# An FNet layer with a gated MLP on one core: a new order of products at the end, x added by DMA, and two jobs of MLP1 moved

## The chip, the core and the metric

The kernel runs on one core of a Trainium2 chip. The core has TensorE for matmuls (PE in the profile, its weight loads PEld), VectorE (DVE), ScalarE (ACT), GpSimd (POOL) and SyncE (SP), which work on their own instruction lists in parallel and wait for each other through semaphores. SP, ACT and POOL can issue DMA transfers; the letter q behind a name (SPq, ACTq, POOLq) stands for an engine's DMA issues. The metric is the device time of one execution in microseconds (us); lower is better.

## The reference

For an input x of 2048 rows (tokens) and 512 columns:

```python
xn = layernorm(x)                       # over the columns
a, b = xn @ dft_hid_re.T, xn @ dft_hid_im.T
s = dft_seq_re @ a - dft_seq_im @ b     # FNet mixing, [2048, 512]
h = relu(xn @ w1 + b1) ** 2             # w1: [512, 1792]
g = silu(h @ w2 + b2)                   # w2: [1792, 512]
out = x + s * g
```

All of it is in float32.

## The kernel before, in words

Every matmul operand is split into a high and a low part (float32r), and a product is made of three matmuls: high by high, high by low, low by high. ScalarE writes the high part (L125), VectorE the low one by subtraction (L128), which it can do only when ScalarE has finished. On top of that the large products are cut into blocks of two by two and multiplied with seven block products instead of eight (Winograd's form of Strassen's method). Each operand therefore needs sums of its blocks (VectorE, L257 to L269) before its split, and each result needs a few additions of products.

The work runs in four stages: the DFT over the sequence (until about 331 us), the DFT over the columns (Y units, until about 418 us), MLP1 (28 units, until about 561 us) and MLP2 with the gate and the output (until the end).

**MLP1.** Unit n = 0 to 27 makes 256 hidden features for a chunk of 512 tokens: chunk c = n // 7, feature part p = n % 7. A unit has seven products of six matmuls, in the regions A, B, C and D of PSUM (two sets of banks, for even and odd units). TensorE's order overlaps two units; in the loop of unit n it does product 1 of n, products 5 and 4 of n − 1, products 7 and 6 of n, product 3 of n − 1, product 2 of n. ScalarE copies A into B (`seed` "B") and B into C (`seed` "C"), since several results share partial sums. VectorE takes the results from B and C (c22, c21, L775) and squares them (L790); product 3 then adds into region B, so it must wait until c22 has read B. Likewise product 5 adds into B and must wait until ScalarE's seed has copied B to C.

Beside this, VectorE and ScalarE must prepare the operands of later units. Each such job is a generator with a letter and a number, and one call of `go` makes its next step: V (a part of w1: load, sums, split), x (normalized tokens of a chunk, half 0 or 1: load, normalization L610 and sums, split), w (a part of w2), m (the rows of mean and scale for a chunk), h (hidden features back from DRAM as operand of MLP2), l (a load). The table `H_SIDE` says for each unit which steps are called at which of three places: before c22 and c21 of the unit before (first), behind them (second), and at the unit's end (later). An engine runs its instructions strictly in the order in which they were written, so the table sets what stands behind what on VectorE, ScalarE and SP.

**MLP2.** For each chunk of 512 tokens, seven products (banks m1 to m7) are summed over the parts p = 0 to 6 (`outer`, L811). For the last chunk product 4 has two banks of its own, one for each half of its columns (`m4[0]`, `m4[1]`). A part's operand g is made by `operand` in one of three buffers by turns, so a new one waits until TensorE has used the one three parts ago. `REST` says from which part on the last chunk's products are kept for the end, to be done product by product, so that the results come one after another: C11 (from products 1, 2), C22 (1, 2, 6, 7, 5), C12 and C21, each 256 by 256, in a tile z of 128 partitions. Each result then goes through `silu` (ScalarE), `times` (VectorE, with s from the first stages, kept in DRAM and loaded by `load_fin`) and `plus` (VectorE, adds x, and SP sends it out). For the first chunks two of the four results get x in another way: `finish` issues a DMA from POOL's queue that adds x from DRAM onto the tile in SBUF (`accum_op=ALU.add`, L846), and `put` (L849) sends the tile out once that DMA is done.

In the last chunk before the change, x is added to C12 by POOL instead of VectorE (L863 with `eng=nc.gpsimd`), and C21 is finished in two halves.

Of the kernel before, what the change touches and what calls it, by code (L numbers as in the profile page):

```python
# [9 lines left out]
F32R = mybir.dt.float32r  # L10
AF = mybir.ActivationFunctionType
ALU = mybir.AluOpType

P = 128
S, D, F = 2048, 512, 1792
NS, ND, NF = S // P, D // P, F // P
NJ, NP = NS // 2, NF // 2
CW = 256
NC = S // CW
TC = 512  # L20
NTC = S // TC
# [2 lines left out]

ASIDE = 4.2

REST = NP - 3

W1_EARLY = (0, 1)
W2_LATE = (4, 5)  # L30
# [25 lines left out]
H_SIDE = {  # L56
    0: ((), ("V2", "x2"), ("x3",)),
    1: (("V4",), ("V3",), ("V5",)),
    2: ((), ("V4", "V5"), ("V6",)),
    3: ((), ("x3", "V5"), ("m2",)),  # L60
    4: ((), ("V6", "x2"), ("x4",)),
    5: ((), ("V6", "x3"), ("w4",)),
    6: ((), ("x3",), ("x5",)),
    7: (("w4",), ("w4",), ("w5",)),
    8: ((), ("x4",), ()),
# [10 lines left out]
    21: (("h1",), (), ()),  # L76
    22: (("w1",), ("h0",), ("w2",)),
    23: ((), ("h1",), ("w3",)),
    24: (("w2",), ("w1",), ("w6", "h2")),
    25: (("w3",), ("w2",), ("h3", "l4")),  # L80
    26: (("w6",), ("w3",), ("l5",)),
    27: (("h2",), (), ()),
}
ACT_PAIR = (7, 10, 13, 15, 17, 18, 19, 20, 26)
O_SIDE = {0: (("h4",), ("h5",)), 1: ((), ("w6",))}
# [28 lines left out]
C21, C11, C22, C12 = range(4)  # L114
# [5 lines left out]
def fnet_gated_kernel(ctx, tc, x, xt, ct, wd, w1, w2, b1, b2, out):  # L120
    nc = tc.nc
# [8 lines left out]
    def split(*parts):  # L130
        split_hi(*parts)
        split_lo(*parts)
# [211 lines left out]
    one, two = slice(0, 1), slice(1, 2)  # L344
# [112 lines left out]
    g = plain_parts(0, 1)  # L457
# [7 lines left out]
    for j in range(1, NJ):  # L465
# [15 lines left out]
        g = plain_parts(*order[j + 1])  # L481
# [62 lines left out]
    for n, s in enumerate(steps):  # L544
        c, j = s
        if j == 0:
            ms = {k: bank(tag, f"m{k}_{c}") for k, tag in
                  {1: "bb", 2: "b20", 6: "b21", 3: "b30", 5: "b31", 7: "b32", 4: ("ba", "bc")[c % 2]}.items()}
        g = part.pop(s)
# [22 lines left out]
        if j == NJ - 1:  # L572
            e = buf("e", [P, 2048], f"c{c}")
# [9 lines left out]
    xT, W1, W2, fin, ready = {}, {}, {}, {}, {}  # L583
# [83 lines left out]
    def operand(n):  # L667

        apart = n in (0, 1, 3)
        if apart:  # L670
            x_, t = (buf(f"pq{n % 3}{i}", [P, 4, 256], f"hr{n}_{i}") for i in range(2))
        else:
            e = buf("u" if n % 4 else "wd0", [P, 8, 256], f"hr{n}")
            x_, t = e[:, 4:8], e[:, 0:4]
        nc.sync.dma_start(x_, HD[divmod(n, NP)])
        yield
        sums_rows(t, x_)
        yield
        g = ready[n] = buf(("xc6", "xc7", "xc4")[n % 3], [P, 2, 7, 256], f"g{n}", F32R)
        for s, src in ((slice(0, 4), t), (slice(4, 7), x_[:, 0:3])) if apart else ((slice(0, 7), e[:, 0:7]),):  # L680
            split(g[:, HI, s], g[:, LO, s], src)
        yield

    makers.update(m=load_rows, x=tokens, k=load_w1, l=load_w2, V=make_w1, w=make_w2, h=operand)


# [118 lines left out]
    def outer(m, k, n, cols=(0, 1)):  # L805

        p = n % NP
        a, b = PRODUCTS[k]
        for i in cols:
            for a_, b_ in PASSES:  # L810
                nc.tensor.matmul(m[:, i * 256:(i + 1) * 256], ready[n][:, a_, H_SLOT[a], i * P:(i + 1) * P],  # L811
                                 W2[p][:, b_, b], start=p == 0 and i == 0 and (a_, b_) == (HI, HI) and k not in BIASED,
                                 stop=p == NP - 1 and (a_, b_) == (LO, HI), skip_group_check=True)
# [4 lines left out]
    def at(src, k):  # L818

        h, b = WHERE[k]  # L820
        return src.rearrange("(h k p) (b e) -> h b p k e", h=2, k=2, b=2)[h, b]
# [14 lines left out]
    def finish(c, e, k):  # L836

        if len(fin[c]) > 2 + k // 2:
            silu(e, k)
            times(c, e, k)  # L840
            plus(c, e, k)
            return
        silu(e, k)
        times(c, e, k)
        z = e[:, k].rearrange("p (k e) -> p k e", e=256)
        nc.gpsimd.dma_start(z, at(x[c * TC:(c + 1) * TC], k), accum_op=ALU.add)  # L846

    def put(c, e, k):
        nc.sync.dma_start(at(out[c * TC:(c + 1) * TC], k), e[:, k].rearrange("p (k e) -> p k e", e=256))  # L849

    def silu(e, k, cols=slice(0, 2)):

        z = e[:, k, cols.start * 256:cols.stop * 256]
        nc.scalar.activation(z, z, AF.Silu)

    def times(c, e, k, cols=slice(0, 2)):
        w = slice(cols.start * 256, cols.stop * 256)
        nc.vector.tensor_tensor(e[:, k, w], e[:, k, w], fin[c][k // 2][:, k % 2, w], op=ALU.mult)

    def plus(c, e, k, cols=slice(0, 2), eng=None):  # L860
        w = slice(cols.start * 256, cols.stop * 256)
        z = e[:, k, w]
        (eng or nc.vector).tensor_tensor(z, z, fin[c][2 + k // 2][:, k % 2, w], op=ALU.add)  # L863
        nc.sync.dma_start(at(out[c * TC:(c + 1) * TC], k)[:, cols], z.rearrange("p (k e) -> p k e", e=256))

    go("m0")
# [23 lines left out]
    for u in range(1, NC):  # L890
        n = 2 * u + 2
# [40 lines left out]
    for n in range(NTC * NP):  # L932
# [17 lines left out]
        if n == NTC * NP - 1:  # L950
            ms = Banks(0)
# [22 lines left out]
    for n in range(NTC * NP):  # L974
        c, p = divmod(n, NP)
        last = c == NTC - 1
        if n and not last and p == 0:

            ms = Banks(c)
            for k in (2, 4, 5):  # L980
                bias(ms[k], k)
        elif last and p == 0:

            ms = {k: bank(t, f"m{k}_last") for k, t in
                  {1: "b20", 2: "b21", 6: "b30", 7: "b31", 5: "bb", 3: "ba"}.items()}
            m4 = bank("bc", "m40_last"), bank("b32", "m41_last")
# [5 lines left out]
        def add(k, p):  # L992
            if last and k == 4:
                for i in range(2):
                    outer(m4[i], k, NP * c + p, (i,))
            else:
                outer(ms[k], k, NP * c + p)

        go(*O_SIDE.get(n, ((), ()))[0])
        if n == 1:  # L1000
            for k, i in ((1, 1), (2, 1), (6, 1), (4, 1), (5, 0), (3, 0), (7, 1), (5, 1), (3, 1)):
                add(k, i)
        elif n and (not last or p < REST):
            for k in ORDER if p else FIRST_LAST if last else FIRST:
# [28 lines left out]
    def rest(ks, ps=range(REST, NP)):  # L1033
        for k in ks:
            for f in ps:
                add(k, f)

    def step(to, a, b, op, w=whole):
        nc.vector.tensor_tensor(e[:, to, w], a[:, w], e[:, b, w], op=op)

    rest((1, 2, 6), range(REST, tail))
    rest((1, 2), (tail,))
    nc.scalar.activation(e[:, C21], ms[1], AF.Copy)
    step(C11, ms[2], C21, ALU.add)
    silu(e, C11)
    times(c, e, C11)
    plus(c, e, C11)
    rest((6,), (tail,))
    rest((7,))
    step(C12, ms[6], C21, ALU.add)  # L1050
    step(C21, ms[7], C12, ALU.subtract)
    rest((5,))
    step(C22, ms[5], C21, ALU.add)
    silu(e, C22)
    step(C12, ms[5], C12, ALU.subtract)
    rest((3,))
    for f in range(REST, NP):
        outer(m4[0], 4, NP * c + f, (0,))
    times(c, e, C22)
    step(C12, ms[3], C12, ALU.add)  # L1060
    silu(e, C12)
    plus(c, e, C22)
    step(C21, m4[0], C21, ALU.subtract, w[0])
    silu(e, C21, one)
    for f in range(REST, NP):
        outer(m4[1], 4, NP * c + f, (1,))
    times(c, e, C12)
    plus(c, e, C12, eng=nc.gpsimd)
    step(C21, m4[1], C21, ALU.subtract, w[1])
    silu(e, C21, two)  # L1070
    times(c, e, C21, one)
    plus(c, e, C21, one)
    times(c, e, C21, two)
    plus(c, e, C21, two)

# [42 lines left out]
```

## Time and profile before

| What | Value |
|---|---|
| Device time, median of three runs (lowest to highest) | 705.83 us (705.46 to 707.34) |
| Profiled execution | 707.13 us |
| Its span, from first to last instruction | 705.4 us |
| Granted TensorE clock over the span | 0.998 |
| TensorE busy | 695.8 us (99%) |
| VectorE busy | 606.8 us (86%) |
| ScalarE busy | 357.9 us (51%) |
| Matmuls | 5440 |

A row of the timeline gives the start and the duration in us, the engine, the line of the kernel, the operation, the tile written and the tiles read, the shape and the number of instructions merged into the row. Brackets at its end give the idle time of the engine before it and who ended it. In a row of waits come the waiting engine and line, the releaser, the total, the number of times and the longest. In a row of DMA issues come the queue, the count, the size of one and the time from issue to landing.

### The profile page before, as it was taken

The numbers are of one execution on the slowest core, as the hardware profiler recorded it, in microseconds if no ns is written. First come the engines' busy times: TensorE is split into PE (matmuls) and PEld (weight loads), VectorE is DVE, ScalarE is ACT, GpSimd is POOL, SyncE is SP. The second block draws the span as 40 slices with busy tenths as digits, with TensorE's granted clock in tenths as the row PEclk, the third lists the DMA queues.
The fourth block names the chain that finished last, engine by engine and source line by source line (L and its number), as shares of the span: only waits on it lengthen the run. The fifth ranks groups of instructions, "written<-read, shape, count | busy, mean of one in ns | idle before, by whom it ended". The sixth has DMA issues, their size and how long they took to land.

```text
span 705.4 us, 13138 instructions
## 1 busy us (share of the span) xinstructions
PE 695.8 (99%) x5440; PEld 671.7 (95%) x5440; DVE 606.8 (86%) x848; ACT 357.9 (51%) x474; POOL 6.5 (1%) x9
## 2 busy tenths in 40 slices
PE   9999999999999999999999999999999999999996
PEld 6778889999999999999999999999999999999996
DVE  7999779999988988888898699999648599989896
ACT  4446544444434333344455458677778664444441
POOL 0000000000000000000000000000000000101000
PEclk9999999999999999999999999999999999999999
DMA  8535755667475544276587446587426955666743
GB/s 302 190 109 189 269 203 209 247 214 278 174 282 200 184 163 176 94 281 230 176 297 266 151 168 214 204 318 259 157 119 200 356 163 203 185 204 186 235 143 130
DMA packets 50619, 146.88 MB, mean 208 GB/s; under 512 B 4864, under 2 KB 19200, under 8 KB 49152
## 3 DMA queue, kind: packets, MB, share of 16 engines
q1 hardware_dynamic: 43264, 126.13, 51.6%
q10 hardware_dynamic: 6208, 18.88, 6.8%
q0 software_dynamic: 1088, 1.05, 1.0%
q8 instruction: 42, 0.69, 0.4%
q14 instruction: 17, 0.14, 0.1%
HBM read 99.88 MB, written 46.15 MB: 207 GB/s over the span
## 4 chain that ended last, share of the span: by engine, by line
PE 93%; DVE 4%; DMA 1%; ACT 1%; issue 1%; DVEq 0%; ACTq 0%
PE m L325 33%; PE m_o L811 15%; PE r_B L705 12%; PE r_A L705 8%; PE pq_b L340 8%; PE m_last L811 5%; PE r_C L705 4%; PE r_D L705 4%; PE pq_ba L340 2%; PE pq_bb L340 1%; PE pq_bc L340 1%; DMA w2raw<-in_w 1%; DVE c L306 1%; DVE yg L128 0%; DMA x<-in_x 0%
## 5 line engine op out<-in xcount | busy, mean ns | idle before, releaser
L325 PEld LDWEIGHTS m<-g,xc 128*128 128x128 f32 x2016 | 236.4, 188 | 0.5 <-DVE g L128 0.2
L325 PE MATMUL m<-g,xc 128*128 128x256 f32 x2016 | 236.8, 279 | 0.0
L125 ACT ACTIVATE g<-u 128x1792 fp32r<-128x1792 f32 (+3 forms) x70 | 100.1, 1430 | 145.6 <-PE m L325 55.6
L128 DVE TENSOR_TENSOR g<-u,g 128x1792 fp32r<-128x1792 f32 (+3 forms) x70 | 117.5, 1679 | 27.0 <-ACT g L125 26.8
L811 PE MATMUL m_o<-w,g 128*128 128x256 f32 x882 | 105.8, 282 | 0.0
L811 PEld LDWEIGHTS m_o<-w,g 128*128 128x128 f32 x882 | 105.5, 191 | 0.0
L125 ACT ACTIVATE g<-hr 128x1792 fp32r<-128x1792 f32 (+2 forms) x31 | 47.9, 1556 | 49.5 <-PE m_o L811 31.4
L705 PE MATMUL r_B<-xT,w 128*128 128x256 f32 x504 | 70.3, 283 | 0.8 <-DVE h L775 0.8
L340 PE MATMUL pq_b<-g,xc 128*128 128x512 f32 x240 | 66.8, 397 | 0.2
L705 PEld LDWEIGHTS r_B<-xT,w 128*128 128x128 f32 x504 | 64.4, 190 | 1.4 <-DVE h L775 1.1
L128 DVE TENSOR_TENSOR g<-hr,g 128x1792 fp32r<-128x1792 f32 (+2 forms) x31 | 56.8, 1839 | 7.9 <-ACT g L125 7.9
L340 PEld LDWEIGHTS pq_b<-g,xc 128*128 128x128 f32 x240 | 43.8, 188 | 13.2 <-ACT xc L125 2.3
L705 PE MATMUL r_A<-xT,w 128*128 128x256 f32 x336 | 45.0, 282 | 1.3 <-DVE w L128 1.3
L705 PEld LDWEIGHTS r_A<-xT,w 128*128 128x128 f32 x336 | 42.1, 190 | 1.5 <-DVE w L128 1.5
L705 PE MATMUL r_B<-wdp,yg 128*128 128x256 f32 x288 | 37.5, 283 | 0.2 <-DVE y L715 0.2
L705 PEld LDWEIGHTS r_B<-wdp,yg 128*128 128x128 f32 x288 | 35.6, 190 | 0.6 <-DVE y L715 0.4
L811 PE MATMUL m_last<-w,g 128*128 128x256 f32 x294 | 35.3, 282 | 0.0
L811 PEld LDWEIGHTS m_last<-w,g 128*128 128x128 f32 x294 | 35.2, 191 | 0.0
L257 DVE TENSOR_TENSOR u<-u 128x512 f32<-128x512 f32 x48 | 32.9, 685 | 1.9 <-DMA u<-in_ct 1.9
L128 DVE TENSOR_TENSOR yg<-yraw,yg 128x1792 fp32r<-128x1792 f32 x13 | 26.2, 2020 | 3.8 <-ACT yg L125 3.8
L306 DVE TENSOR_TENSOR c<-m,c 128x512 f32<-128x512 f32 x42 | 27.2, 685 | 1.7 <-PE m L325 1.0
L125 ACT ACTIVATE yg<-yraw 128x1792 fp32r<-128x1792 f32 x13 | 22.1, 1697 | 6.6 <-DVE yraw L266 5.2
(172 smaller groups left out, 865.4 us busy)
## 6 DMA issues: line engine op xcount, KB each, us to landing
u<-in_ct SPq DMA_DIRECT2D x63, 512.0 KB, 3.6
hd<-h ACTq DMA_DIRECT2D x28, 512.0 KB, 4.1
hr<-hd SPq DMA_DIRECT2D x28, 512.0 KB, 3.7
wdp<-wdd SPq DMA_DIRECT2D x8, 896.0 KB, 6.5
yraw<-pqd SPq DMA_DIRECT2D x13, 512.0 KB, 5.1
pqd<-c SPq DMA_DIRECT2D x6, 1024.0 KB, 4.0
y<-y ACTq DMA_DIRECT2D x8, 512.0 KB, 4.3
fin<-y SPq DMA_DIRECT2D x16, 256.0 KB, 5.1
```

What stands on the lines that cost most here:

```text
L125: nc.scalar.activation(hi, src, AF.Copy)
L128: nc.vector.tensor_tensor(lo, src, hi.bitcast(F32), op=ALU.subtract)
L257: nc.vector.tensor_tensor(t[:, 0:2], r[:, 0:1].to_broadcast([P, 2, 256]), r[:, 1:3], op=ALU.add)
L306: nc.vector.tensor_tensor(part_(to), m, part_(frm), op=op)
L325: nc.tensor.matmul(ps[:, d], w[:, a_, d * P:(d + 1) * P], halves(mv(b_)), start=first and d == 0 and (a_, b_) == (HI, HI), stop=last and ( ...
L340: nc.tensor.matmul(accs[c][k], w, part[c, j][:, b_, 2 * h:2 * h + 2], start=j == 0 and h == 0 and (a_, b_) == (HI, HI), stop=j == NJ - 1 a ...
L705: nc.tensor.matmul(self.region(REGION[k]), w, mv, start=i == 0 and k in (1, 7), stop=i == len(ops) - 1, skip_group_check=True)
L811: nc.tensor.matmul(m[:, i * 256:(i + 1) * 256], ready[n][:, a_, H_SLOT[a], i * P:(i + 1) * P], W2[p][:, b_, b], start=p == 0 and i == 0 an ...
```

## The change

Four things change.

1. `REST` goes from `NP - 3` to `NP - 4`: in the last chunk the products of parts 3, 4, 5 and 6 are kept for the end. Four operands live at once then, so the last one gets a fourth buffer (wd0). For parts 3 to 5 the products 1, 2, 6, 7 and 5 are done part by part, then part 6 product by product, then products 3 and 4.
2. C11 and C22 of the last chunk get x by an accumulating DMA from POOL (`add_x`); they are sent out later by `put`, C11 by SP's queue and C22 by ScalarE's. C12 gets x from VectorE; POOL makes no addition any more.
3. For the second half of C21, the earlier result is subtracted from the bank `m4[1]` in PSUM (VectorE) while product 4's last part is still missing; TensorE adds that part afterwards, and ScalarE takes silu straight from the bank.
4. `H_SIDE`: in units 2 to 5, x3's normalization moves to unit 2, weight part 6 (V6) does its sums and its split in unit 4, before x2's split, and the rows m2 are loaded a unit earlier. In units 24 to 27 the steps of w2's parts move from the first place to the second, behind the split of the part before.

```diff
-REST = NP - 3
+REST = NP - 4
...
 H_SIDE = {
-    2: ((), ("V4", "V5"), ("V6",)),
-    3: ((), ("x3", "V5"), ("m2",)),
+    2: ((), ("V4", "V5", "x3"), ("V6", "m2")),
+    3: ((), ("V5",), ()),
...
-        g = ready[n] = buf(("xc6", "xc7", "xc4")[n % 3], [P, 2, 7, 256], f"g{n}", F32R)
+        g = ready[n] = buf("wd0" if n == NTC * NP - 1 else ("xc6", "xc7", "xc4")[n % 3], [P, 2, 7, 256], f"g{n}", F32R)
...
+    def add_x(c, e, k):
         z = e[:, k].rearrange("p (k e) -> p k e", e=256)
         nc.gpsimd.dma_start(z, at(x[c * TC:(c + 1) * TC], k), accum_op=ALU.add)
...
-    rest((1, 2, 6), range(REST, tail))
+    def rest4(i, ps):
+        for f in ps:
+            outer(m4[i], 4, NP * c + f, (i,))
+
+    for f in range(REST, tail):
+        rest((1, 2, 6, 7, 5), (f,))
     rest((1, 2), (tail,))
     nc.scalar.activation(e[:, C21], ms[1], AF.Copy)
     step(C11, ms[2], C21, ALU.add)
     silu(e, C11)
+    rest((6, 7, 5), (tail,))
+    step(C12, ms[6], C21, ALU.add)
     times(c, e, C11)
-    plus(c, e, C11)
-    rest((6,), (tail,))
-    rest((7,))
-    step(C12, ms[6], C21, ALU.add)
+    add_x(c, e, C11)
     step(C21, ms[7], C12, ALU.subtract)
-    rest((5,))
     step(C22, ms[5], C21, ALU.add)
     silu(e, C22)
     step(C12, ms[5], C12, ALU.subtract)
+    times(c, e, C22)
+    add_x(c, e, C22)
     rest((3,))
-    for f in range(REST, NP):
-        outer(m4[0], 4, NP * c + f, (0,))
-    times(c, e, C22)
     step(C12, ms[3], C12, ALU.add)
     silu(e, C12)
-    plus(c, e, C22)
+    rest4(1, range(REST, tail))
+    nc.vector.tensor_tensor(m4[1][:, w[1]], m4[1][:, w[1]], e[:, C21, w[1]], op=ALU.subtract)
+    put(c, e, C11)
+    times(c, e, C12)
+    plus(c, e, C12)
+    rest4(0, range(REST, NP))
+    rest4(1, (tail,))
     step(C21, m4[0], C21, ALU.subtract, w[0])
     silu(e, C21, one)
-    for f in range(REST, NP):
-        outer(m4[1], 4, NP * c + f, (1,))
-    times(c, e, C12)
-    plus(c, e, C12, eng=nc.gpsimd)
-    step(C21, m4[1], C21, ALU.subtract, w[1])
-    silu(e, C21, two)
+    nc.scalar.activation(e[:, C21, w[1]], m4[1][:, w[1]], AF.Silu)
     times(c, e, C21, one)
     plus(c, e, C21, one)
+    put(c, e, C22, nc.scalar)
     times(c, e, C21, two)
     plus(c, e, C21, two)
```

Three places show how the order moves. The first is VectorE in units 2 to 4. In the rows, w1raw is a raw part of w1 with its sums, w_5 and w_6 are split parts, xr_4455 is x3 (in xs are its sums), xT_4680 and xT_4744 are x2's split operand, and each h tile holds two units' results (h_4559 and h_4561: units 2 and 3). Before, from the sums of part 5 on:

```order
L266 TENSOR_TENSOR w1raw_4519<-w1raw_4519 128x256
L775 SCALAR_TENSOR_TENSOR h_4559<-r_B,b1s,h_4559 128x256
L775 SCALAR_TENSOR_TENSOR h_4559<-r_C,b1s,h_4559 128x256
L790 SCALAR_TENSOR_TENSOR h_4559<-h_4559 128x2x256
L610 TENSOR_TENSOR xr_4455<-xr_4455,rows_4191 128x1024 x2
L128 TENSOR_TENSOR w_5_4613<-w1raw_4519,w_5_4613 128x1792
```

And after the change:

```order
L266 TENSOR_TENSOR w1raw_4519<-w1raw_4519 128x256
L610 TENSOR_TENSOR xr_4455<-xr_4455,rows_4191 128x1024 x2
L775 SCALAR_TENSOR_TENSOR h_4561<-r_B,b1s,h_4561 128x256
L775 SCALAR_TENSOR_TENSOR h_4561<-r_C,b1s,h_4561 128x256
L790 SCALAR_TENSOR_TENSOR h_4561<-h_4561 128x2x256
L128 TENSOR_TENSOR w_5_4618<-w1raw_4519,w_5_4618 128x1792
```

The two L610 of x3 now stand ahead of unit 2's c22, c21 and square.

The second place is ScalarE in unit 4. Its rows begin with the seed of B for unit 4 and c11 of unit 3 (L763); `h<-r_D` is unit 4's copy of product 7, `r_C<-r_B` its seed of C. Before:

```order
L135 ACTIVATE r_B<-r_A 128x256
L763 ACTIVATE h_4559<-r_A,b1s 128x256
L125 ACTIVATE xT_4680<-xr_4244 128x768
L125 ACTIVATE xT_4680<-xs_4414 128x1024
L135 ACTIVATE h_4692<-r_D 128x256
L135 ACTIVATE r_C<-r_B 128x256
```

And after:

```order
L135 ACTIVATE r_B<-r_A 128x256
L763 ACTIVATE h_4561<-r_A,b1s 128x256
L125 ACTIVATE w_6_4680<-w1raw_4586 128x1792
L135 ACTIVATE h_4690<-r_D 128x256
L135 ACTIVATE r_C<-r_B 128x256
```

The split of part 6, which reads sums that VectorE makes in the same unit behind unit 3's c22, c21 and square, now stands ahead of unit 4's copy and seed; x2's split moves a unit back.

The third place is VectorE in unit 24 (h_5826 holds unit 23's results, w2raw_1_5852 the sums of w2's part 2, w_1 the split of part 1). The difference, with the rows of before marked by − and those of after by +:

```order
+L775 SCALAR_TENSOR_TENSOR h_5826<-r_B,b1s,h_5826 128x256
+L775 SCALAR_TENSOR_TENSOR h_5826<-r_C,b1s,h_5826 128x256
+L790 SCALAR_TENSOR_TENSOR h_5826<-h_5826 128x2x256
+L128 TENSOR_TENSOR w_1_5943<-w2raw_5298,w_1_5943 128x1792
 L257 TENSOR_TENSOR w2raw_1_5852<-w2raw_0_5851 128x512
 L258 TENSOR_TENSOR w2raw_1_5852<-w2raw_1_5852,w2raw_0_5851 128x256
 L259 TENSOR_TENSOR w2raw_1_5852<-w2raw_1_5852,w2raw_0_5851 128x256
-L775 SCALAR_TENSOR_TENSOR h_5826<-r_B,b1s,h_5826 128x256
-L775 SCALAR_TENSOR_TENSOR h_5826<-r_C,b1s,h_5826 128x256
-L790 SCALAR_TENSOR_TENSOR h_5826<-h_5826 128x2x256
-L128 TENSOR_TENSOR w_1_5946<-w2raw_5298,w_1_5946 128x1792
```

The sums of part 2 now come behind unit 23's steps and the split of part 1.

At the end of the program POOL has two more L849 transfers in the place of its addition, each waiting only for loads and for VectorE's multiply of its tile.

More of the change, by code (lines that the diff above doesn't have):

```diff
@@ L58 @@
     1: (("V4",), ("V3",), ("V5",)),
-    2: ((), ("V4", "V5"), ("V6",)),
-    3: ((), ("x3", "V5"), ("m2",)),
-    4: ((), ("V6", "x2"), ("x4",)),
-    5: ((), ("V6", "x3"), ("w4",)),
+    2: ((), ("V4", "V5", "x3"), ("V6", "m2")),
+    3: ((), ("V5",), ()),
+    4: ((), ("V6", "V6"), ("x4", "w4")),
+    5: ((), ("x2", "x3"), ()),
     6: ((), ("x3",), ("x5",)),
@@ L78 @@
     23: ((), ("h1",), ("w3",)),
[L79 to L82, printed above, removed]
+    24: ((), ("w1", "w2"), ("w6", "h2")),
+    25: ((), ("w2", "w3"), ("h3", "l4")),
+    26: ((), ("w3", "w6"), ("l5",)),
+    27: ((), ("h2",), ()),
 }
@@ L844, in finish, with put @@
         times(c, e, k)
+        add_x(c, e, k)
+    def add_x(c, e, k):
         z = e[:, k].rearrange("p (k e) -> p k e", e=256)
         nc.gpsimd.dma_start(z, at(x[c * TC:(c + 1) * TC], k), accum_op=ALU.add)
-    def put(c, e, k):
-        nc.sync.dma_start(at(out[c * TC:(c + 1) * TC], k), e[:, k].rearrange("p (k e) -> p k e", e=256))
+    def put(c, e, k, queue=nc.sync):
+        queue.dma_start(at(out[c * TC:(c + 1) * TC], k), e[:, k].rearrange("p (k e) -> p k e", e=256))
     def silu(e, k, cols=slice(0, 2)):
@@ L858, in times, with plus @@
         nc.vector.tensor_tensor(e[:, k, w], e[:, k, w], fin[c][k // 2][:, k % 2, w], op=ALU.mult)
-    def plus(c, e, k, cols=slice(0, 2), eng=None):
+    def plus(c, e, k, cols=slice(0, 2)):
         w = slice(cols.start * 256, cols.stop * 256)
         z = e[:, k, w]
-        (eng or nc.vector).tensor_tensor(z, z, fin[c][2 + k // 2][:, k % 2, w], op=ALU.add)
+        nc.vector.tensor_tensor(z, z, fin[c][2 + k // 2][:, k % 2, w], op=ALU.add)
         nc.sync.dma_start(at(out[c * TC:(c + 1) * TC], k)[:, cols], z.rearrange("p (k e) -> p k e", e=256))
```

## The prediction

> **What bounds the kernel now.** I read the page's busy shares first, then the waits of TensorE, then the timeline of the three places where the change moves work: early MLP1, late MLP1 and the end.
>
> ```profile
> PE 695.8 (99%) x5440; PEld 671.7 (95%) x5440; DVE 606.8 (86%) x848; ACT 357.9 (51%) x474; POOL 6.5 (1%) x9
> PE r_A L705 <- DVE w L128: 1.3, 1, 1.3
> 664.25 35.25 PE L811 MATMUL m_last<-w,g 128*128 128x256 f32 x294
> ```
>
> TensorE is busy 695.8 of 705.4 us and the change neither adds nor removes a matmul. So it can move the time only by TensorE's waits in MLP1 (the wait above, and one on r_B shown further down, lie in the units that the table reorders) and by what runs after the last matmul. The last row gives the pace: 35.25/294 = 0.12 us a matmul, 0.72 for a product of six, 5.04 for a unit of 42.
>
> **Early MLP1, before.** All rows are the timeline's: start, duration, engine, line.
>
> ```profile
> 430.03 0.42 DVE L266 TENSOR_TENSOR w1raw<-w1raw 128x256 f32<-128x256 f32 x1
> 430.37 0.48 DVE L775 SCALAR_TENSOR_TENSOR h<-r_B,b1s,h 128x256 f32<-128x256 f32 x1
> 431.31 1.60 PE L705 MATMUL r_B<-xT,w 128*128 128x256 f32 x12
> 432.08 2.48 DVE L610 TENSOR_TENSOR xr<-xr,rows 128x1024 f32<-128x1024 f32 x2
> 434.48 2.02 DVE L128 TENSOR_TENSOR w<-w1raw,w 128x1792 fp32r<-128x1792 f32 x1
> 438.12 0.69 DVE L263 TENSOR_TENSOR w1raw<-w1raw 128x512 f32<-128x512 f32 x1
> 439.30 0.42 DVE L266 TENSOR_TENSOR w1raw<-w1raw 128x256 f32<-128x256 f32 x1
> 439.23 0.88 PE L705 MATMUL r_B<-xT,w 128*128 128x256 f32 x6
> 440.17 1.70 ACT L125 ACTIVATE w<-w1raw 128x1792 fp32r<-128x1792 f32 x1
> 441.76 0.38 ACT L135 ACTIVATE h<-r_D 128x256 f32<-128x256 f32 x1
> 445.43 0.74 PE L705 MATMUL r_A<-xT,w 128*128 128x256 f32 x4 [1.32 <-DVE w L128]
> 450.99 0.87 PE L705 MATMUL r_B<-xT,w 128*128 128x256 f32 x6
> ```
>
> See here that VectorE works back to back, one piece behind TensorE, and that TensorE then starves once, at 445.43, for weight 6. From product 5 of unit 4 (439.23) to that of unit 6 (450.99) are 11.76 us, where two units need 10.08: 1.68 lost.
>
> *Step 1, x3's normalization moved ahead of unit 2's c22.* The two L610 take 434.48 − 432.08 = 2.40 of VectorE. c22, at 430.37 before, comes at 432.77 and ends at 433.25. TensorE's product 3 of unit 2, the second half of the twelve at 431.31, is due at 432.03 and adds into the bank that c22 reads; it starts at 433.30: +1.27. Behind it ScalarE's c12, square and seed shift alike, which nobody else is short of.
>
> *Step 2, weight 6 summed and split in one unit.* The sums still stand behind unit 3's three steps, so they run at 438.23 to 439.84 (0.1 later than before). But ScalarE's split of weight 6 now stands at ScalarE's place of 435, and waits for the sums until 439.88, then takes 1.70. Queued behind it are the m7 copy (0.26 to 0.36 a step) and unit 4's seed of C from B, which would end near 442.15. TensorE's product 5 of unit 4 overwrites B and must wait for that seed: due at 439.23 + 1.27 = 440.50, it starts at 442.2, +1.70. VectorE idles meanwhile (439.84 to 441.6) and the split's low part ends at 443.55.
>
> *Step 3, what is gained.* Weight 6 is needed at 446.5 now, so the 1.68 go. x3's operand is later, 451.45 for the first half by the same durations; unit 7 asks for it at 452.0, with 0.5 to spare. From product 5 of unit 4 on: 442.2 + 10.08 = 452.28 against 450.99. Steps 1 to 3: **+1.29**. Bounds: −1.68 if ScalarE's and VectorE's lateness is absorbed, +1.9 if x3's second half (452.6) is what unit 7 waits for; I take the worked value, the only one with every row behind it.
>
> The moved loads (rows of chunk 2, x4) reach SP's queue in the same order; x4's load waits for a split that is 5 us later, but is read only in unit 8, behind all of this: 0.
>
> **Late MLP1.**
>
> ```profile
> 535.95 0.88 PE L705 MATMUL r_B<-xT,w 128*128 128x256 f32 x6
> 537.69 0.69 DVE L257 TENSOR_TENSOR w2raw<-w2raw 128x512 f32<-128x512 f32 x1 [1.89 <-DMA w2raw<-in_w]
> 539.22 0.48 DVE L775 SCALAR_TENSOR_TENSOR h<-r_B,b1s,h 128x256 f32<-128x256 f32 x1
> 539.75 0.98 PE L705 MATMUL r_B<-xT,w 128*128 128x256 f32 x6 [0.76 <-DVE h L775]
> 552.40 0.87 PE L705 MATMUL r_B<-xT,w 128*128 128x256 f32 x6
> ```
>
> The sums of weight 2 wait for their load (until 537.69) ahead of c22, and TensorE waits for c22. *Step 4* puts the sums behind c22 and the previous split. c22 then runs when product 5 is done, 536.9, and the sums at 540.7, after the load. From 535.95 to 552.40 are 16.45 us for three units, which need 15.12: **−1.33**, if nothing new is late. I checked the next one: the c22 of units 24 and 25 would start at 542.2 and 547.5, due by 543.4 and 548.4. Bounds 0 and −1.5 (a further short wait).
>
> MLP1 in sum: −0.04.
>
> **The end, before.**
>
> ```profile
> 682.02 2.02 DVE L128 TENSOR_TENSOR g<-hr,g 128x1792 fp32r<-128x1792 f32 x1
> 686.21 2.03 DVE L128 TENSOR_TENSOR g<-hr,g 128x1792 fp32r<-128x1792 f32 x1 [0.84 <-ACT g L125]
> 691.64 0.69 DVE L858 TENSOR_TENSOR z<-z,fin 128x512 f32<-128x512 f32 x1 [0.70 <-DMA out<-z]
> 692.37 0.69 DVE L863 TENSOR_TENSOR z<-z,fin 128x512 f32<-128x512 f32 x1
> 692.98 1.48 DVE L1039 TENSOR_TENSOR z<-m_last,z 128x512 f32<-128x512 f32 x2
> 699.54 0.43 DVE L1039 TENSOR_TENSOR z<-m_last,z 128x256 f32<-128x256 f32 x1
> 699.70 1.26 POOL L863 TENSOR_TENSOR z<-z,fin 128x512 f32<-128x512 f32 x1 [56.62 <-DVE z L858]
> 699.88 1.35 DVE L858 TENSOR_TENSOR z<-z,fin 128x256 f32<-128x256 f32 x1
> 702.07 0.42 DVE L863 TENSOR_TENSOR z<-z,fin 128x256 f32<-128x256 f32 x1
> out<-z SPq DMA_DIRECT2D x2, 128.0 KB, 1.8
> out<-z SPq DMA_DIRECT2D x1, 256.0 KB, 2.1
> out<-z SPq DMA_DIRECT2D x15, 256.0 KB, 3.7
> ```
>
> The last 128 KB leave at 702.5, land 1.8 later, at 704.3, and the span ends 1.1 after that. The 1.35 of a multiply that elsewhere takes 0.42 lies under POOL's addition: 0.93 lost to it.
>
> *Step 5, the products' order.* Units 3 to 6 now stay for the end; the rest starts after three units, 664.25 + 126 × 0.12 = 679.4, and ends at 699.5 as before. The operands are split as before: the third of the four (row at 682.02) is done at 684.0 and needed at 686.5; the last, whose new buffer needn't wait for unit 3's products, is done at 687.3, a little before the 688.2 of the row at 686.21, and needed at 690.2. No wait: 0.
>
> *Step 6, the last quarter.* From a step to one that depends on it are 0.73 (691.64 to 692.37), to one that doesn't 0.61 (to 692.98); with these VectorE's list gives: c11 at 691.7 (product 2 done at 691.6), times(C11) 693.1 to 693.8, times(C22) 695.8 to 696.5, C12's last step 696.7, the subtraction in PSUM 697.8 to 698.2 (no such write is in the trace; the step that reads PSUM took 0.43, one of 512 columns 0.74, and its bank is asked for only at 699.15, so TensorE waits in neither case), C12 done at 699.55, then both halves of C21 (ScalarE's silu straight from PSUM is ready before VectorE is), the last ending at 702.05 instead of 702.49. The gain of the addition taken from POOL is mostly spent on C12's addition, which VectorE now does. By this chain alone the end is at 705.0, −0.44.
>
> *Step 7, x added by DMA.* The four accumulating transfers of the trace:
>
> ```profile
> 600.74 1.29 DVE L858 TENSOR_TENSOR z<-z,fin 128x512 f32<-128x512 f32 x2
> 601.74 1.34 POOL L846 DMA_DIRECT2D z<-in_x  x1 [601.29 <-DVE z L858]
> 606.91 1.22 POOL L846 DMA_DIRECT2D z<-in_x  x1 [3.84 <-DVE z L863]
> 636.88 1.21 POOL L846 DMA_DIRECT2D z<-in_x  x1 [28.75 <-DVE z L858]
> 641.85 1.23 POOL L846 DMA_DIRECT2D z<-in_x  x1 [3.76 <-DVE z L858]
> z<-in_x POOLq DMA_DIRECT2D x1, 256.0 KB, 4.9
> z<-in_x POOLq DMA_DIRECT2D x1, 256.0 KB, 4.6
> DMA to landing us min/median/max: 4.6/5.0/5.3
> ```
>
> The second of a pair waits, by the program, only for its multiply, done at 602.03; yet it is issued at 606.91, when the first (601.74 + 4.9 = 606.64) has landed. The other pair reads the same: 636.88 + 4.6 = 641.48, next issue 641.85. So two transfers of this size don't overlap: the second starts 0.3 after the first's landing. At the end: first issue 693.8 + 0.3 = 694.1, landing 4.75 later at 698.85; second issue 699.15 (not at 696.8, when its data is ready), landing about 5.0 later, 704.15, with the last outputs beside it. Only then may ScalarE's queue send C22 out: 704.25, landing 2.15 later at 706.4, end of span 707.5 against 705.4: **+2.1**. SP's queue loses nothing: its wait for C11 ends at 698.9, before C12 is ready. Bounds: 4.6 twice, 0.27 and 2.1 give +1.4; 5.3 twice and a slightly crowded output give +3.2.
>
> The Trainium skill, page "DMA: Bandwidth & Descriptors", section "Anatomy of one DMA — SWDGE (gpsimd) path", prices such a transfer at about 2.0 us plus its bytes over 436 GB/s, an estimate of 2.6 us here; by it both would have landed by 699.6, step 6 would end last, and the sum would be −0.5, 705.3. The trace disagrees: 4.6 to 5.3 from issue to landing.
>
> **Sum.** −0.04 + 2.1 = +2.0 on the profiled execution's 707.13 (its span 705.4); the same on the median 705.83, which lies lower by 1.3: **707.8**. 0.3%, about what a measurement of this kernel tells from no change, is 2.1 us, so the forecast lies just below that line.
>
> **Rivals.** *A, the second transfer starts while the first flies.* Against it stand both pairs. It would issue at 696.8, land at 701.8, its output at 704.05: tail −0.2, 705.6, not slower. It decides as soon as the second issue stands before 698. *B, ScalarE doesn't block at step 2* (the sums come early enough): MLP1 gives about 1.7 more, 706.1; without step 1's wait as well 704.8. For it speaks that VectorE is short of time only by little; against it the back-to-back rows, which leave no room to run earlier. *C, the end is more crowded:* a second landing of 5.3 and an output of 3.7, the median of all such outputs: 699.15 + 5.3 + 0.1 + 3.7 + 1.1 = 709.35 for the span, +3.9, so 709.7. *D, without other traffic an accumulating transfer is as quick as an output of its size,* 2.1: the second lands at 698.9, its output before 703, and step 6 ends last: 705.3. Against it stand all four landings, though loads ran beside them. This is the case that the skill's page comes near to.
>
> **Chances.** Forecast 0.62, its own range 706.9 to 709.0, half on each side of 707.95; A 0.14 (same); B 0.10 (0.06 same, 0.04 faster); C 0.11 (slower); D 0.03 (same). So faster 0.04, same 0.54, slower 0.42. The range 705.4 to 709.5 holds the forecast, A, half of B and part of C.
>
> **What would show it.** A TensorE wait of 1.3 on r_B by L775 near 433 and one of 1.7 near 442 by ScalarE's copy; no wait on weight 6 and none near 539. POOL's second L849 some 5 us after the first, near 699; the last DMA issued by ScalarE near 704; last VectorE step near 702. The prediction is wrong if that second issue follows its multiply, or if the matmuls of m_last don't run through without a gap.

## The result, and the profile after

The changed kernel takes **709.18 us** (median of 11 runs, 708.20 to 710.01) where the kernel before takes 705.83 (median of 11 runs, 705.20 to 709.08). The ratio is 1.0039, with a 95% interval of 1.0026 to 1.0051: 1.8 to 3.6 us slower. The medians differ by 3.35; the means, 706.32 and 709.07, differ by 2.75, since four of the eleven runs of the kernel before lie 1 us or more above its median. The forecast was 707.8, +2.0: both its sign and its two main mechanisms came out, but against the medians its size is too small by about the gain that it had counted for late MLP1.

The profiled execution took 709.78 us, its span is 708.0. From the page and the waits of TensorE, after:

```profile
PE 695.2 (98%) x5440; PEld 671.8 (95%) x5440; DVE 605.5 (86%) x847; ACT 357.5 (50%) x474; POOL 7.6 (1%) x10
PE r_B L705 <- ACT r_C L135: 1.5, 1, 1.5
PE r_B L705 <- DVE h L775: 1.1, 1, 1.1
```

TensorE's waits of before in MLP1, 1.3 on weight 6 and 0.8 near 539, are not in this list, and two others stand in their place. Early MLP1 in the timeline, after:

```profile
430.95 2.48 DVE L610 TENSOR_TENSOR xr<-xr,rows 128x1024 f32<-128x1024 f32 x2
433.34 0.48 DVE L775 SCALAR_TENSOR_TENSOR h<-r_B,b1s,h 128x256 f32<-128x256 f32 x1
433.87 0.98 PE L705 MATMUL r_B<-xT,w 128*128 128x256 f32 x6 [1.09 <-DVE h L775]
440.07 0.42 DVE L266 TENSOR_TENSOR w1raw<-w1raw 128x256 f32<-128x256 f32 x1
440.53 1.70 ACT L125 ACTIVATE w<-w1raw 128x1792 fp32r<-128x1792 f32 x1 [3.35 <-DVE w1raw L266]
442.40 0.38 ACT L135 ACTIVATE r_C<-r_B 128x256 f32<-128x256 f32 x1
442.83 0.98 PE L705 MATMUL r_B<-xT,w 128*128 128x256 f32 x6 [1.51 <-ACT r_C L135]
452.93 0.87 PE L705 MATMUL r_B<-xT,w 128*128 128x256 f32 x6
```

The first wait is the chain L610, c22, product 3. The second is the chain sums (until 440.49), ScalarE's split of weight 6, which had stood waiting for 3.35 us, seed of C, product 5 of unit 4. Product 5 of unit 2 starts at 429.74 here and at 429.15 before, that of unit 6 at 452.93 and 450.99: after the 0.59 by which this execution was late already, early MLP1 costs 1.35.

Late MLP1, after (product 5 of unit 23, unit 23's c22, product 5 of unit 26):

```profile
537.88 0.88 PE L705 MATMUL r_B<-xT,w 128*128 128x256 f32 x6
538.87 0.48 DVE L775 SCALAR_TENSOR_TENSOR h<-r_B,b1s,h 128x256 f32<-128x256 f32 x1 [1.13 <-PE r_B L705]
552.99 0.87 PE L705 MATMUL r_B<-xT,w 128*128 128x256 f32 x6
```

Here VectorE waits for TensorE and not the other way round, and the three units take 15.11 us: 1.34 less than the 16.45 of the execution profiled before.

The end, after, in the timeline, and its accumulating transfers and ScalarE's output among the DMA issues:

```profile
664.64 35.15 PE L811 MATMUL m_last<-w,g 128*128 128x256 f32 x294
693.45 0.69 DVE L861 TENSOR_TENSOR z<-z,fin 128x512 f32<-128x512 f32 x1
694.56 1.21 POOL L849 DMA_DIRECT2D z<-in_x  x1 [51.29 <-DVE z L861]
696.24 0.69 DVE L861 TENSOR_TENSOR z<-z,fin 128x512 f32<-128x512 f32 x1
699.12 1.22 POOL L849 DMA_DIRECT2D z<-in_x  x1 [3.36 <-DVE z L861]
701.86 0.42 DVE L866 TENSOR_TENSOR z<-z,fin 128x256 f32<-128x256 f32 x1
704.54 0.42 ACTq L852 DMA_DIRECT2D out<-z  x1
z<-in_x POOLq DMA_DIRECT2D x1, 256.0 KB, 4.3
z<-in_x POOLq DMA_DIRECT2D x1, 256.0 KB, 5.4
out<-z ACTq DMA_DIRECT2D x1, 256.0 KB, 2.2
```

C22's multiply ends at 696.93, its transfer is issued at 699.12, when C11's has landed (694.56 + 4.3 = 698.86). It lands 5.4 later, and only then ScalarE's queue sends C22 out. VectorE had been done at 702.28. The last matmul ends at 699.79 (664.64 + 35.15), the span 8.2 later; before it was 5.9 (699.50 and 705.4). The end costs 2.3.

The terms together: 0.59 of the start, + 1.35, − 1.34, − 0.30 between unit 26 and the last matmul, + 2.31 at the end give the +2.6 by which the two spans differ. But these are two single executions: that of before was 1.30 above its median, that of after 0.60 above its own. The experiments show which of the terms belong to the kernels and which to the execution.

### The profile page after: what moved, and what is told of

Its sections match the earlier page's. It is cut to its first block, busy times and chain, and to the rows that moved or that the text cites. A ratio compares the mean times of both kernels' runs of the same rounds, so it can differ in the third digit from the quotient of the medians.

```text
span 708.0 us, 13135 instructions
## 1 busy us (share of the span) xinstructions
PE 695.2 (98%) x5440; PEld 671.8 (95%) x5440; DVE 605.5 (86%) x847; ACT 357.5 (50%) x474; POOL 7.6 (1%) x10
## 4 chain that ended last, share of the span: by engine, by line
PE 93%; DVE 4%; ACT 1%; issue 1%; DMA 0%; ACTq 0%; DVEq 0%
PE m L325 33%; PE m_o L811 15%; PE r_B L705 13%; PE r_A L705 8%; PE pq_b L340 8%; PE m_last L811 5%; PE r_C L705 4%; PE r_D L705 4%; PE pq_ba L340 2%; PE pq_bc L340 1%; PE pq_bb L340 1%; DVE c L306 1%; DVE yg L128 0%; DMA x<-in_x 0%; DVE bn L185 0%
```

## The experiments

Three runs each did one part of the change alone, to price it; the others take one suspected cause away. Where rounds were timed, the ratio is to runs of the kernel before on the same chip.

### Early MLP1 alone, late MLP1 alone, the end alone

Early MLP1: the kernel before with the four rows of the table for units 2 to 5.

```diff
-    2: ((), ("V4", "V5"), ("V6",)),
-    3: ((), ("x3", "V5"), ("m2",)),
-    4: ((), ("V6", "x2"), ("x4",)),
-    5: ((), ("V6", "x3"), ("w4",)),
+    2: ((), ("V4", "V5", "x3"), ("V6", "m2")),
+    3: ((), ("V5",), ()),
+    4: ((), ("V6", "V6"), ("x4", "w4")),
+    5: ((), ("x2", "x3"), ()),
```

> The kernel before with only the four H_SIDE rows of units 2 to 5 of the change. Main theory: x3's normalization ahead of unit 2's c22 and ScalarE's wait for weight 6's sums make two TensorE waits, on r_B by L775 of 1.1 and on r_B by ScalarE's copy of 1.5, and the wait of 1.3 on r_A goes; from product 5 of unit 4 on the net is +1.3 us, so about 707.1. Rival (the reordering costs nothing by itself, the waits come with the rest of the change): 705.8, with the old wait on r_A.

Measured: 706.75 us, ratio 1.0018 (1.0007 to 1.0030), which is +1.3 us (+1.1 by the medians). Both waits are there, 1.1 behind VectorE's c22 and 1.5 behind ScalarE's seed, and the one on weight 6 is gone. From product 5 of unit 2 to that of unit 6 TensorE takes 23.18 us (428.83 to 452.01) instead of 21.84, +1.34. Steps 1 to 3 of the prediction are confirmed, in kind and in sum.

Late MLP1: the kernel before with the rows for units 24 to 27.

```diff
-    24: (("w2",), ("w1",), ("w6", "h2")),
-    25: (("w3",), ("w2",), ("h3", "l4")),
-    26: (("w6",), ("w3",), ("l5",)),
-    27: (("h2",), (), ()),
+    24: ((), ("w1", "w2"), ("w6", "h2")),
+    25: ((), ("w2", "w3"), ("h3", "l4")),
+    26: ((), ("w3", "w6"), ("l5",)),
+    27: ((), ("h2",), ()),
```

> The kernel before with only the four H_SIDE rows of units 24 to 27 of the change. Main theory: TensorE's wait of 0.8 near 540 goes, with the smaller ones behind it, -1.3 to -1.6 us, so about 704.3. Rival (the late load of weight 2 is only met later): no gain, 705.8, and a wait on r_B by L775 remains.

Measured: 705.55 us, ratio 0.9999 (0.9990 to 1.0009). The order meant to cure the wait near 539 brings nothing measurable. Either the wait is paid back later, or it isn't there in most executions.

The end: the changed kernel with the table of before.

> The changed kernel with the H_SIDE table of before: only the new order of the end, the accumulating transfers and the sum in PSUM. Main theory: the end of the span comes 8.2 us behind the last matmul instead of 5.9, all of it in the second accumulating transfer's late issue and C22's output, so +2.3, about 708.1; MLP1 as before. Rival (the cost lies in the operands of the four last units): a wait of TensorE on m_last, and the second transfer issued near its multiply.

Measured: 707.91 us, ratio 1.0032 (1.0020 to 1.0044), +2.3 us. POOL issues its transfers at 692.93 and 697.66, 4.7 apart, and the span ends 8.2 us behind the last matmul. This is step 7 in its full size.

The parts that cost, 1.0018 and 1.0032, make 1.0050 together, just inside the interval of the whole change.

### Is the wait near 539 there in the kernel before?

In the two runs above whose late rows are those of before (early alone, end alone) the wait is missing too: product 5 goes from unit 23 to unit 26 in 15.11 us. So the kernel before was run once more, unchanged.

> The kernel before, unchanged, once more. Theory (the TensorE wait of 0.76 near 539, on VectorE's sums behind a late load of weight 2, belongs to the one execution that the first profile shows): no such wait here, the three units of late MLP1 take 15.1 us instead of 16.45, and the time is about 705.8 instead of 707.1. Rival (the wait is there in most executions): the wait and the 16.4 us come again.

Measured: 705.75 us. Product 5 of units 23 and 26 and the sums of weight 2, in the timeline of this run:

```profile
535.86 0.68 DVE L257 TENSOR_TENSOR w2raw<-w2raw 128x512 f32<-128x512 f32 x1
536.09 0.88 PE L705 MATMUL r_B<-xT,w 128*128 128x256 f32 x6
551.20 0.87 PE L705 MATMUL r_B<-xT,w 128*128 128x256 f32 x6
```

The sums start right behind VectorE's step before them, without the 1.89 of waiting for the load that the first profile shows at 537.69, and the three units take 15.11. The load was issued at 531.35 here and at 531.20 there. Here it is a row of the DMA issues; in the first profile's chain of waits it has a row of its own, the four columns being start, duration, engine and what it did:

```profile
w2raw<-in_w SPq DMA_DIRECT2D x1, 512.0 KB, 4.3
531.20 6.46 DMA w2raw<-in_w
```

In one of the four executions profiled with these rows of the table the load took 6.5 us, in the other three 4.3. One of these three is the same program. So the wait of 0.76, and the gain of 1.33, belong to an execution in which this load is slow, and the median isn't such a one.

That doesn't make the slow load a thing of one execution. Of the nine profiles with the new rows, it is slow in three that stand further down: 6.5 us in the run with halves, 6.6 in that with only C22 cut, 7.0 in the last version. There the sums stand behind c22, and nothing waits. In the last version's timeline (product 5 of units 23 and 26, unit 23's c22, the sums), with the load from its DMA issues:

```profile
w2raw<-in_w SPq DMA_DIRECT2D x1, 512.0 KB, 7.0
535.52 0.88 PE L705 MATMUL r_B<-xT,w 128*128 128x256 f32 x6
536.52 0.48 DVE L775 SCALAR_TENSOR_TENSOR h<-r_B,b1s,h 128x256 f32<-128x256 f32 x1 [1.13 <-PE r_B L705]
540.23 0.68 DVE L257 TENSOR_TENSOR w2raw<-w2raw 128x512 f32<-128x512 f32 x1
550.63 0.87 PE L705 MATMUL r_B<-xT,w 128*128 128x256 f32 x6
```

The three units take 15.11 us here as well. So the new order does what step 4 says, but only in executions in which the load is slow. The timed runs fit this: of 85 of the kernel before (in five groups, each beside runs of other kernels) 21 lie 1.0 us or more above the median of their group; of 65 of the kernels with the new rows, one does. None of these 22 was profiled, so it isn't shown that the load is what made them longer; why it is slow at times isn't known either.

### What makes the second accumulating transfer wait?

By the program it waits for its multiply alone. Two causes fit the traces: POOL takes such transfers one at a time, or the room that the kernel sets aside for POOL's transfers (`dynamic_dma_scratch_size=1024`, bytes of SBUF per partition) has no place for a second one. The first experiment doubles the room; to make place for it in SBUF, only the first 256 values of b2 are kept, and used for all columns.

```diff
-    nc = bacc.Bacc("TRN2", target_bir_lowering=False, num_devices=1, dynamic_dma_scratch_size=1024)
+    nc = bacc.Bacc("TRN2", target_bir_lowering=False, num_devices=1, dynamic_dma_scratch_size=2048)
```

> The changed kernel with twice the room for POOL's transfer descriptors (2048 bytes a partition instead of 1024); to make place, the bias b2 of the second 256 columns is left out (that of the first is used for both). Theory R (the room holds one transfer of 256 KB): the second is issued some 0.4 us behind its multiply, about 2.6 us behind the first, and the span ends 5.6 to 5.9 behind the last matmul instead of 8.2. Theory O (accumulating transfers go one at a time, whatever the room): the second is issued 4.5 behind the first as now, and the end stays 8.2 behind the last matmul.

POOL's issues at the end of this run, in the timeline:

```profile
694.27 1.21 POOL L848 DMA_DIRECT2D z<-in_x  x1 [54.83 <-DVE z L860]
697.05 1.20 POOL L848 DMA_DIRECT2D z<-in_x  x1 [1.57 <-DVE z L860]
```

They are 2.8 apart instead of 4.6, the second right behind its multiply while the first flies; the last matmul ends at 699.56 and the span at 705.4, 5.8 later instead of 8.2. The one run took 707.12 us. The pairs of the first chunks, too, are now issued without a gap (from 601.89 and from 636.97 on). The room was the cause; that such transfers go one at a time whatever the room is refuted.

The same with the room as it was, but each of the last chunk's two transfers cut in two:

```diff
-        nc.gpsimd.dma_start(z, at(x[c * TC:(c + 1) * TC], k), accum_op=ALU.add)
+        src = at(x[c * TC:(c + 1) * TC], k)
+        for i in range(2 if c == NTC - 1 else 1):
+            cut = slice(i, i + 1) if c == NTC - 1 else slice(0, 2)
+            nc.gpsimd.dma_start(z[:, cut], src[:, cut], accum_op=ALU.add)
```

> The changed kernel, with each of the two accumulating transfers of the last chunk issued as two of 128 KB. Theory R (the descriptor room holds 256 KB of such transfers, and a new one waits until room is free): the two halves of C11 are issued one straight behind the other, without a landing between; the halves of C22 follow as C11's land; the span ends 6.5 to 8.2 us behind the last matmul. Theory O (one accumulating transfer at a time): four landings in a row, the halves some 3.5 us or more apart, the span ends 13 us or more behind the last matmul.

```profile
694.14 1.80 POOL L852 DMA_DIRECT2D z<-in_x  x2 [51.05 <-DVE z L864]
696.92 1.76 POOL L852 DMA_DIRECT2D z<-in_x  x2 [0.98 <-DVE z L864]
```

The one run took 707.13 us; the span ends 5.9 behind the last matmul. That is better than expected: C22's first half is issued at 696.92, before even the first half of C11 has landed (694.14 + 3.2 = 697.3). So three halves fit into the room, although two wholes don't; a room of one whole transfer, as the expectation had it, is too small a guess. The last experiment on this cuts only C22's transfer:

```diff
-        nc.gpsimd.dma_start(z, at(x[c * TC:(c + 1) * TC], k), accum_op=ALU.add)
+        src = at(x[c * TC:(c + 1) * TC], k)
+        halves = c == NTC - 1 and k == C22
+        for i in range(2 if halves else 1):
+            cut = slice(i, i + 1) if halves else slice(0, 2)
+            nc.gpsimd.dma_start(z[:, cut], src[:, cut], accum_op=ALU.add)
```

> The changed kernel with C11's accumulating transfer whole and only C22's in two halves. If the room is counted in descriptors and holds between one and a half and two transfers of 256 KB: C22's first half is issued at its multiply, 2.8 us behind C11's issue and before C11 lands, the second half waits for C11's landing, some 4.8 us behind C11's issue; the span ends about 7 us behind the last matmul. If a whole transfer shuts out every other until it lands: both halves wait, the first is issued some 4.8 us behind C11's issue, and the span ends 7.5 us or more behind the last matmul.

```profile
693.88 1.21 POOL L853 DMA_DIRECT2D z<-in_x  x1 [50.98 <-DVE z L865]
696.57 0.90 POOL L853 DMA_DIRECT2D z<-in_x  x1 [1.48 <-DVE z L865]
698.61 0.88 POOL L853 DMA_DIRECT2D z<-in_x  x1 [1.14 <-issue]
z<-in_x POOLq DMA_DIRECT2D x1, 256.0 KB, 4.4
```

The one run took 707.47 us; the span ends 6.6 behind the last matmul. One and a half transfers fit: the first half of C22 follows its multiply, 2.7 behind C11's issue. Two don't: the second half comes at 698.61, 0.3 behind C11's landing (693.88 + 4.4 = 698.28), and the profile names nothing that it waited for. The Trainium skill, page "DMA: Bandwidth & Descriptors", section "SWDGE vs HWDGE vs iDMA", says that POOL's transfers are written as pairs of descriptors into rings in a part of SBUF set aside for them; the runs agree with a room that fills up, and none of them shows what is counted in it.

Last, the end without a second transfer: C11 by DMA, C22 by VectorE's addition, as before the change.

```diff
-    add_x(c, e, C22)
+    plus(c, e, C22)
...
-    put(c, e, C22, nc.scalar)
```

> The changed kernel, but only C11 of the last chunk gets x by an accumulating transfer; C22 gets it from VectorE's addition and leaves by SP's queue, as before. Main theory (the second accumulating transfer waits for the first one's landing, and nothing else at the end costs): the span ends 5.7 to 6.2 us behind the last matmul instead of 8.2; time 709.2 - 2.2 = 707.0, ratio to before 1.0017; MLP1's waits of 1.5 and 1.1 stay. Rival (the reordered end is itself longer, by the subtraction in PSUM or VectorE's fuller list): the span ends 7 us or more behind the last matmul, time 708.2 or more.

Measured: 707.17 us, ratio 1.0019 (1.0009 to 1.0029); the span ends 6.0 behind the last matmul (663.85 + 35.15 = 699.00; 705.0). The rest of the new end, with its subtraction in PSUM and its fuller VectorE, costs nothing and wins nothing against the 5.9 of before.

### The second wait of early MLP1

In the changed kernel, weight 6's sums a unit earlier than its split again:

```diff
-    3: ((), ("V5",), ()),
-    4: ((), ("V6", "V6"), ("x4", "w4")),
+    3: ((), ("V5", "V6"), ()),
+    4: ((), ("V6",), ("x4", "w4")),
```

> The changed kernel, but weight 6 is summed in unit 3 behind weight 5's split and only split in unit 4. Main theory (ScalarE, blocked behind the sums, makes the 1.5 us wait on r_B by ScalarE's copy of step 2): that wait goes to under 0.3, VectorE's c22 of unit 3 starts about 438.6 where 439.0 is due, time 709.2 - 1.4 = 707.8, ratio 1.0028; the 1.1 of step 1 stays. Rival (VectorE has no time to spare in these units, so its lateness comes back at the next step that somebody waits for): the 1.5 becomes a wait of about 1 on VectorE's c22 or on x3's split, time 708.8 or more, ratio 1.0042.

Measured: 707.61 us, ratio 1.0022 (1.0012 to 1.0032), 1.6 us under the changed kernel's median. The wait of 1.5 is gone, that of 1.1 stays, and no new wait of TensorE is in the list. From product 5 of unit 2 to that of unit 6 are 21.55 us (429.19 to 450.74), where the changed kernel takes 23.19 and the one before 21.84. So the cause was ScalarE, blocked behind the sums. And VectorE is less full than its unbroken rows had suggested: with the 1.1 of x3's normalization still in, this order is already 0.3 ahead of that of before.

### A version that beats both

This pointed to an order for early MLP1 without either wait: x3's normalization goes behind weight 6's split. The end keeps the two halves, and C22 leaves half by half. Against the changed kernel with the halves:

```diff
-    2: ((), ("V4", "V5", "x3"), ("V6", "m2")),
-    3: ((), ("V5",), ()),
-    4: ((), ("V6", "V6"), ("x4", "w4")),
-    5: ((), ("x2", "x3"), ()),
+    2: ((), ("V4", "V5"), ("V6",)),
+    3: ((), ("V5", "V6"), ()),
+    4: ((), ("V6", "x3"), ("m2", "x4")),
+    5: ((), ("x2", "x3"), ("w4",)),
...
-    put(c, e, C22, nc.scalar)
+    for i in range(2):
+        half = slice(i, i + 1)
+        z = e[:, C22].rearrange("p (k e) -> p k e", e=256)
+        nc.scalar.dma_start(at(out[c * TC:(c + 1) * TC], C22)[:, half], z[:, half])
```

> The changed kernel with two things mended. Early MLP1: x3's normalization stands behind weight 6's split in unit 4, weight 6 is summed behind weight 5's split in unit 3. End: the halves of the run before, and C22 sent out half by half. Main theory (VectorE has time in these units if no step stands ahead of a c22 that is due, and the end is set by VectorE's last step once the accumulating transfers overlap): waits of 0.4 to 0.8 in units 5 to 7 in place of the 1.68 of the kernel before, span end 5.4 to 5.9 us behind the last matmul; 705.8 - 0.9 - 0.3 = 704.6, ratio 0.998. Rival (VectorE is full in these units, whatever the order): waits of 1.6 or more in sum and a time of 705.5 to 706, ratio 1.000.

Measured: 706.07 us, ratio 1.0003 (0.9994 to 1.0011): about the rival's time, but not by its cause. From unit 2 to unit 6 it takes 21.12 us (428.82 to 449.94), 0.72 less than before, as hoped. Then this, VectorE and TensorE in unit 7:

```profile
452.10 0.69 DVE L257 TENSOR_TENSOR w2raw<-w2raw 128x512 f32<-128x512 f32 x1 [1.42 <-DMA w2raw<-in_w]
453.62 0.48 DVE L775 SCALAR_TENSOR_TENSOR h<-r_B,b1s,h 128x256 f32<-128x256 f32 x1
454.16 0.97 PE L705 MATMUL r_B<-xT,w 128*128 128x256 f32 x6 [1.22 <-DVE h L775]
```

It is a wait like that of 539, this time made by the order. Weight 4 is part 4 of w2 (w4 in the table). Its load stands in SP's queue behind the rows of chunk 2 and behind x4, which wait for VectorE's later steps; it was issued at 444.59 only, beside those loads, and took 7.5 us to land. The buffer had been free since VectorE's split of weight 6 ended at 439.2. So the load goes first:

```diff
-    4: ((), ("V6", "x3"), ("m2", "x4")),
-    5: ((), ("x2", "x3"), ("w4",)),
+    4: ((), ("V6", "x3"), ("w4", "m2")),
+    5: ((), ("x2", "x3"), ("x4",)),
```

> The run before, with weight 4's load ahead of chunk 2's rows in SP's queue, and x4's load one unit later. Main theory (what was gained in units 5 to 7, 0.7 us, went to a TensorE wait of 1.2 behind weight 4's late load, and to nothing else): weight 4 lands before 449, VectorE's sums of it start without a wait at about 450.7, no TensorE wait above 0.6 in units 5 to 8; 706.07 - 1.2 = 704.9, ratio 0.9987. Rival (VectorE is full, so unit 7 waits all the same): a wait of 0.8 or more on VectorE in unit 7 or 8, time 705.6 or more, ratio 0.9997 or more.

Measured: **704.54 us** (median of 12 runs), ratio to before **0.9980** (0.9971 to 0.9988), 1.1 us by the medians. Weight 4's load is issued at 439.88 and takes 4.0 us, and its sums wait for nothing. All of TensorE's waits that its profile shows, product 5 of units 2 and 6, and the end:

```profile
PE pq_b L340 <- ACT xc L125: 1.4, 1, 1.4
PE warm L443 <- DVE idle L439: 1.2, 1, 1.2
PE r_B L705 <- DVE y L715: 0.2, 1, 0.2
429.45 0.88 PE L705 MATMUL r_B<-xT,w 128*128 128x256 f32 x6
450.57 0.87 PE L705 MATMUL r_B<-xT,w 128*128 128x256 f32 x6
662.28 35.15 PE L811 MATMUL m_last<-w,g 128*128 128x256 f32 x294
```

No wait of MLP1 is left in the list; some 1.0 us of short ones, which the waits don't name, remain between units 2 and 6 (21.12 us, where four units of 5.04 take 20.16). Early MLP1 gives 0.72 against before, and the end, 5.8 behind the last matmul (697.43 and 703.2), about 0.1; the other 0.3 of the medians isn't traced.

## Why the prediction was right, and where it was wrong

- **Steps 1 to 3, early MLP1: right.** The forecast waits of 1.27 and 1.70 came as 1.1 and 1.5, at the places and by the releasers named; the wait on weight 6 went. From product 5 of unit 2 to that of unit 4 they cost 3.01 (13.09 us where two units need 10.08), forecast 2.97; from unit 4 to unit 6 nothing is lost any more (10.10). Net +1.35 in the trace and +1.34 in the trace of this part alone, against +1.29. Rival B, in which ScalarE doesn't block, fell: it stood waiting for 3.35 us.
- **Step 4, late MLP1: right as a mechanism, wrong as a term of the sum, and this is the miss.** The step that failed is the one from the profiled execution to the median: the −1.33 was carried over unchanged ("the same on the median 705.83, which lies lower by 1.3"). The row that carried it, sums waiting 1.89 for a load, comes only when that load takes 6.5 us; in the three other profiles with the same rows it took 4.3, and the three units took 15.11. This part alone gives 0.9999, no gain. The remark that this execution lay 1.3 above the median was the hint: the wait near 539 and the excess are of one size. That the trace after shows 1.34 less, as forecast, is luck: its load took 4.4, so the old order, which didn't wait at 4.3, would hardly have waited either. What the new order does is seen in the three profiles in which the load took 6.5 to 7.0 and nothing waited.
- **The number.** Without step 4 the forecast's own terms, +1.29 and +2.1, give 709.2, which is the median measured. With it the forecast, 707.8, stood just under the line of 2.1 us between no change and slower, and the result above it. 709.18 lies outside the 706.9 to 709.0 that the forecast gave itself, and inside 705.4 to 709.5 only because that range was stretched for rivals; rival C's 709.7 is near in number, but its mechanism didn't come.
- **Step 5, the products' order: right.** m_last runs through without a gap, 35.15 us against 35.25.
- **Step 6, VectorE's last quarter: right, and without effect, as the sum had it.** VectorE's last step ends 2.49 behind the last matmul (702.28 and 699.79), forecast 2.55. But the gain of 0.44 wouldn't have come even without step 7: in the run with halves VectorE's last step ends 2.49 behind the last matmul as well, and the span still ends 5.9 behind it, as before. The last output of 128 KB landed 2.2 us after its issue there, with C22's output issued 0.4 us ahead of it, where that of before took 1.7; that C22's output is the reason isn't shown.
- **Step 7, the accumulating transfers: right, a little small.** Issues 4.6 apart against 5.05, landings of 4.3 and 5.4 against 4.75 and 5.0, ScalarE's output at 704.54 against 704.25. +2.3 against +2.1. What the prediction left open is the cause: it is the room for POOL's transfers, which the second pair of experiments shows.
- **The rivals.** A, the second transfer starting while the first flies, fell; it is what a room of 2048 bytes makes of the same code. Of C, the crowded end, the second landing came (5.4, where C has 5.3), but not what carried its price: ScalarE's output took 2.2 and not 3.7. D, a quick transfer, fell: alone at the end, in the run with one transfer, it took 4.7. The estimate of 2.6 from the Trainium skill's page "DMA: Bandwidth & Descriptors", section "Anatomy of one DMA — SWDGE (gpsimd) path", fell with it for these accumulating transfers; even the halves took 3.0 or more.

## What to carry to other kernels

A wait that ends on a DMA's landing, in one profiled execution that is slower than the median by the size of that wait, is no term of a sum on the median: look for the same rows in a second execution before a gain is built on it, and count it only for the share of executions that have it. In a strict queue, a step brought forward costs what is queued behind it as soon as its own input is late, so move the producer first and the load ahead of it. Here two accumulating transfers from POOL's queue overlapped only while their room lasted: cut the transfers, or enlarge the room, before work is taken from an engine and given to them.

## What the hardware showed beside

At 1024 bytes per partition POOL's room took one and a half accumulating transfers of 256 KB but not two; at 2048 it took two. Cut in halves, they didn't cost more: each half took 0.9 of issuing on POOL (1.2 for a whole), landed 3.0 us or more after its issue, 3.5 in the median (the two whole ones of the changed kernel took 4.3 and 5.4), and the end of the span came 2.3 us earlier against the last matmul, with no byte less moved. And one load of 512 KB, that of w2's part 2 in late MLP1, took 6.5 to 7.0 us in four of the thirteen profiled executions and 4.3 to 4.7 in the nine others; it cost TensorE time only where the sums of it stood ahead of c22, 1.3 us in the first profile.
